# Seven block products in place of eight for the output projection of token tile pairs, in a fused attention and gMLP kernel

## The chip, the cores and the metric

The kernel runs on one core of a Trainium2 chip. Its time is device microseconds of one launch; the median of three runs is compared.

## The reference, cut to what matters

Two blocks follow each other on 2048 tokens of 1024 features. The first is a layer norm, a QKV projection, a sliding attention over eight keys two tokens apart, and an output projection, with a residual. The second is a gated MLP that mixes tokens; the change lies there:

```python
h = x + _A_ref(_layernorm(x), A_wqkv, A_wo)
z = _gelu(einsum('bsd,df->bsf', _layernorm(h), w_in))   # 2 * 1792 features
z1 = z[..., :Fh]
z2 = _layernorm(z[..., Fh:])
g = einsum('ts,bsf->btf', w_sp, z2) + b_sp[None, :, None]
out = h + einsum('bsf,fd->bsd', z1 * g, w_out)          # (2048 x 1792) @ (1792 x 1024)
```

Everything is bf16 at the interface. `w_sp` is 2048 x 2048, `w_out` 1792 x 1024.

## The kernel before

TensorE, ScalarE (ACT), VectorE (DVE) and GpSimd (POOL) run in the order in which the kernel issues their instructions. Up to the last Gelu that order comes from a planner, the class `Order`, which is given operations with estimated costs, dependencies and buffer slots. From there on (line 1087) it is written out by hand, and so is the order of SyncE's (SP) loads.

The planned part makes, among other things, `z1` and the normalised `z2` and stores them in DRAM. `b_z1` (line 851) evicts an accumulator of two PSUM banks through the Gelu on ACT (L867). Three accumulators, tag `acc`, take six of the eight PSUM banks; the attention's pool `ps_att` has the other two. `row_sum` (L899) takes the sums of magnitudes of the rows of `w_sp` on ACT, with an accumulator; `row_scales` (L903 to L908) makes a power of two from each, by which the rows are scaled so that they can be held in fp16, and `rinv`, the factor that undoes it at the end. `load_raw` loads `w_sp` transposed, `scale_raw` (L941) scales it to fp16.

The hand-written part goes over two passes `pr`, each for 1024 output tokens. A pass has a group stage and an output stage.

- Group stage: seven groups `i`, each for two tiles of 128 features. A group makes `g` for them as one 2 x 2 block product with seven instead of eight products. The forms of `w_sp` (sums and differences of blocks) come from `t_forms` (L948 to L954, 4096 elements a partition each), once for each pass; the forms of `z2` from `z_form` (L971, 1024 elements each), four for each group, built on VectorE one group ahead. `times` (L1071) issues eight matmuls of 512 columns; a group has four products into fresh banks `k1`, `k4`, `k3`, `k2`, and three that go on in `k1`, `k4` and `k3`: 56 matmuls. ACT copies the first three out half way (`p1`, `p7`, `p5`); GpSimd adds `p7 + p5` (L1116) and later three more (L1145, L1146, L1150); VectorE makes `u` (L1144) and the rest (L1149 to L1154) and multiplies by `z1`, loaded as `z1c`. The result is `zg`, 14 feature tiles by 1024 tokens, bf16.
- In pass 0 the groups also carry loads: the rows of `w_sp` for pass 1 (`wn`, two buffers), `w_out` in two pieces on GpSimd's queue (`wout_a` in group 4, `wout_b` in group 5), the next z2 (`z2f`), and the transposed `w_sp` of pass 1. In group 5 one transpose on TensorE (L1131) turns the row scales of pass 1.
- Output stage: eight token tiles `il`. Each makes 14 x 2 matmuls of 512 columns of `zg` with `w_out` (`project`, L1169) into two banks; VectorE scales by `rinv`, adds `h` and writes the output tile `hr` (L1172). Pass 0 has `scale_raw`, `t_forms` and `z_form` for pass 1 between the tiles on VectorE. The last tile of pass 1 is cut into 512, 384 and 128 columns.

All banks of this part come from one pool `psq` of eight. TensorE's first matmul in it waits for the last Gelu.

Of the kernel before, what the change touches and what calls it, by code (L numbers as in the profile page):

```python
# [13 lines left out]
I32 = mybir.dt.int32  # L14
# [118 lines left out]
def kernel(  # L133
# [48 lines left out]
    rinv = cpool.tile([P, NT], I32, name="rinv_w")  # L182

# [49 lines left out]
    with tc.manual_schedule(engines={mybir.EngineType.SP}):  # L233
# [10 lines left out]
        dma(csb[:], consts_d.ap()[:, :])  # L244
        load_pair(2)
# [133 lines left out]
    ps_att = att_stack.enter_context(tc.tile_pool(name="ps_att", bufs=1, space=PSUM))  # L379
# [471 lines left out]
    def b_z1(c):  # L851
        for fp in range(NF // 2):
# [12 lines left out]
            def ev(fp=fp):  # L865
                z1s = l1.tile([P, 2, CH], BF16, name="z1s", tag="xn", bufs=4)
                A.activation(z1s[:], G["accy", c, fp][:], ACTF.Gelu_apprx_tanh)  # L867
                last_store[:] = [(A.dma_start if c == NCH - 1 else dma)(z1_d[2 * fp:2 * fp + 2, :, c * CH:(c + 1) * CH].rearrange("f p s -> p f s"), z1s[:])]
# [24 lines left out]
    def load_wn(i, pool, tag, bufs):  # L893
        wn[i] = pool.tile([P, S], BF16, name="wn", tag=tag, bufs=bufs)
        A.dma_start(wn[i][:], B_w_sp[i * P:(i + 1) * P, :])
# [5 lines left out]
    def row_scales(pr):  # L901
        n = slice(pr * TPP, (pr + 1) * TPP)
        V.tensor_tensor(wlim[:, n], wabs[:, n, 0], wabs[:, n, 1], op=ALU.add)  # L903
        V.tensor_scalar(wlim[:, n], wlim[:, n], 2.0 ** -40, 2.0 ** 60, op0=ALU.max, op1=ALU.min)
        V.tensor_scalar(wexp[:, n], wlim[:, n].bitcast(I32), 0x7F800000, None, op0=ALU.bitwise_and)
        V.tensor_scalar(rsc[:, n], wexp[:, n], -1.0, float(266 << 23), op0=ALU.mult, op1=ALU.add)
        V.tensor_scalar(rinv[:, n], wexp[:, n], float(-(12 << 23)), None, op0=ALU.add)
        V.tensor_copy(rsc16[:, n], rsc[:, n].bitcast(FP32))  # L908

# [102 lines left out]
    def close_():  # L1012
        sp_hand.__enter__()
        att_stack.close()
        zpools["z"] = ctx.enter_context(tc.tile_pool(name="zpool", bufs=1, side="right"))

# [5 lines left out]
    rs_ = add("DVE", 1.0, lambda: row_scales(0), [G["avdone", NCH - 1]] + wabs_ops, prio=2.8)  # L1022
# [34 lines left out]
    psq = ctx.enter_context(tc.tile_pool(name="psq", bufs=8, space=PSUM))  # L1057

    for _ in range(7):
        psq.tile([P, CH], FP32, name="bank", tag="bank", bufs=8)  # L1060

    def bank():
        return psq.tile([P, CH], FP32, name="bank", tag="bank", bufs=8)
# [5 lines left out]
    def times(dst, wts, mov, first):  # L1069
        for k in range(HK):  # L1070
            T.matmul(dst[:], wts[:, k, :], mov[:, k, :], start=(first and k == 0), stop=(k == HK - 1), skip_group_check=not first)  # L1071
# [14 lines left out]

    for pr in range(NCH // 2):
# [5 lines left out]
        for i in range(NQ):  # L1093
# [8 lines left out]
            if i == 0:  # L1102
                zg = p2.tile([P, NF, 2 * CH], BF16, name="zg", tag="zg", bufs=1)
            z1c = z1cs[n]
            k1, k4, k3, k2 = bank(), bank(), bank(), bank()
            times(k1, a11, b11, True)
            A.copy(p1[:], k1[:])  # L1107
            times(k4, zs[n, 3], t3, True)
            A.copy(p7[:], k4[:])
            times(k3, zs[n, 1], t1_, True)  # L1110
            A.copy(p5[:], k3[:])
            times(k2, zs[n, 2], t2_, True)
            times(k1, a12, b21, False)
            times(k4, a22, t4_, False)
            times(k3, zs[n, 4], b22, False)
            nc.gpsimd.tensor_tensor(p7[:], p7[:], p5[:], op=ALU.add)  # L1116
            if pr == 0:
# [4 lines left out]
                if i <= 3:  # L1122
                    for t in (TPP + 2 * i, TPP + 2 * i + 1):
                        load_wn(t, p2, "wn", 2)
                if i == 4:
                    dma_w(wout_a[:], wout_view[:, 0:8, :])
                elif i == 5:
                    dma_w(wout_b[:], wout_view[:, 8:NF, :])
                    row_scales(1)
                    rps = psq.tile([P, 2 * CH], BF16, name="rpq", tag="bank", bufs=8)  # L1130
                    T.transpose(rps[0:TPP, 0:P], rsc16[:, TPP:NT], ident[:])  # L1131
                    A.copy(rscT[0:TPP, :], rps[0:TPP, 0:P])
                    A.dma_start(rs_d[TPP:NT, :], rscT[0:TPP, :])
            if i + 1 < NQ:
                for m in (3, 1, 2, 4):
                    z_form(n + 1, m)
            if n + 2 < 2 * NQ:
# [17 lines left out]
            if i == NQ - 2:  # L1155
                for il in range(3):
                    load_hr(2 * pr * TPC + il)
        for il in range(2 * TPC):
            t = 2 * pr * TPC + il
            if pr == 0 and il == 0:  # L1160
                load_raw(3)
                bias_in(1, p2, "z1c", 2)
            if il + 3 < 2 * TPC:
                load_hr(t + 3)
            hr = hrs[t]

            def project(outs, lo, hi, f):
                wt, f0 = (wout_a, f) if f < 8 else (wout_b, f - 8)
                T.matmul(outs, zg[:, f, il * P:(il + 1) * P], wt[:, f0, lo:hi], start=(f == 0), stop=(f == NF - 1))  # L1169

            def finish_(lo, hi, acc):
                V.scalar_tensor_tensor(hr[:, lo:hi], acc[:, 0:hi - lo], rv[:, t:t + 1], hr[:, lo:hi], op0=ALU.mult, op1=ALU.add)  # L1172

            if t < NT - 1:
                acc = [bank(), bank()]
                for f in range(NF):
                    for nh in range(2):
                        project(acc[nh][:], nh * CH, (nh + 1) * CH, f)
                for nh in range(2):
                    finish_(nh * CH, (nh + 1) * CH, acc[nh])  # L1180
                dma(out2d[t * P:(t + 1) * P, :], hr[:])
            else:
                for n, (lo, hi) in enumerate(LAST_COLS):
                    acc = bank()
# [53 lines left out]
```

## Time and profile before

| | us |
|---|---|
| median of 3 runs (lowest, highest) | 701.23 (700.89, 701.79) |
| the profiled execution, its own time | 701.22 |
| its span | 699.4 |
| TensorE matmuls busy | 693.8 |
| VectorE busy | 508.1 |
| ScalarE busy | 276.6 |
| GpSimd busy | 117.6 |

The table's busy times and the span are of one profiled execution; its own time is 1.8 us longer than its span. Where a row is quoted, its first two numbers are start and length in microseconds from the span's start, then come the engine, the line of the kernel, the operation, and what it writes and reads. PE is TensorE, PEld its weight load. In brackets stands how long the engine was idle before it, and what ended that.

### The profile page before, as it was taken

Reading aid. Unit: us, or ns where it says so; the run is one execution under the profiler, and the core shown is the slowest. Engines: PE = TensorE matmul, PEld = TensorE weight load, DVE = VectorE, ACT = ScalarE, POOL = GpSimd, SP = SyncE. Lnnn points to the kernel's source line nnn. Section 1 sums busy time; section 2 is a strip of 40 time slices with the busy share of each in tenths; the row PEclk is TensorE's granted clock in tenths of the full one; section 3 lists DMA queues with packets and bytes.
Section 4 is the critical chain, followed back from the end, with each engine's and each line's share of the span. In section 5 each row is a group of like instructions: output and inputs, shape, how many; then the busy total and the mean of one; then the engine's idle time right before and its main releaser. Section 6 shows DMA issues by size and latency. Waiting matters only on the chain.

```text
span 699.4 us, 8823 instructions
## 1 busy us (share of the span) xinstructions
PE 693.8 (99%) x3427; PEld 359.4 (51%) x3427; DVE 508.1 (73%) x614; ACT 276.6 (40%) x388; POOL 117.6 (17%) x113
## 2 busy tenths in 40 slices
PE   9999999999999999999999999999999999999998
PEld 7766665566645445444444544444444444444444
DVE  6899899999999799997985177556457845564222
ACT  4547652453238876755673642345100012111000
POOL 0100010011110111100301120424420023435000
PEclk9999999999999999999999999999999999999999
DMA  9968597677993679361864996699995125361121
GB/s 326 328 229 239 173 216 254 152 209 234 250 352 146 185 211 256 135 183 38 178 214 123 233 273 191 194 257 249 321 293 157 57 87 153 96 171 65 46 90 46
DMA packets 145193, 133.04 MB, mean 190 GB/s; under 512 B 68672, under 2 KB 117216, under 8 KB 145024
## 3 DMA queue, kind: packets, MB, share of 16 engines
q1 hardware_dynamic: 132688, 88.93, 45.3%
q0 software_dynamic: 7808, 32.97, 16.7%
q10 hardware_dynamic: 4656, 10.59, 4.7%
q8 instruction: 27, 0.44, 0.2%
q14 instruction: 14, 0.11, 0.1%
HBM read 75.24 MB, written 33.10 MB: 155 GB/s over the span
## 4 chain that ended last, share of the span: by engine, by line
PE 99%; ACT 0%; DVE 0%; issue 0%
PE bank L1071 24%; PE acc L461 22%; PE acc L793 14%; PE acc L861 14%; PE bank L1169 14%; PE acc L716 8%; PE acc L303 2%; PE wps L226 1%; PE L L555 0%; PE tpt L299 0%; PE pb L617 0%; ACT z1s L867 0%; ACT xnT L300 0%; DVE hr L1172 0%; PE tpa L299 0%
## 5 line engine op out<-in xcount | busy, mean ns | idle before, releaser
L861 PE MATMUL acc<-hnT,win 128*128 128x512 bf16 x448 | 98.0, 379 | 0.0
L793 PE MATMUL acc<-win,hnT 128*128 128x512 bf16 (+1 forms) x512 | 98.0, 352 | 0.0
L793 PEld LDWEIGHTS <-hnT 128*128 128x128 bf16 x512 | 49.9, 98 | 47.4 <-issue 0.7
L525 DVE TENSOR_TENSOR prod<-qT,kT 128x4096 bf16<-128x4096 bf16 x32 | 72.7, 2283 | 1.4 <-ACT kT L467 1.4
L1169 PEld LDWEIGHTS <-zg 128*128 128x128 bf16 x462 | 44.7, 98 | 52.4
L1071 PEld LDWEIGHTS <-zs 128*128 128x128 f16 x448 | 43.9, 98 | 52.8
L861 PEld LDWEIGHTS <-win 128*128 128x128 bf16 x448 | 43.7, 98 | 52.6 <-issue 0.7
L472 ACT CAST stg<-acc 128x1024 bf16<-128x1024 f32 x36 | 36.4, 1012 | 61.5 <-PE acc L461 52.3
L1107 ACT COPY p<-bank 128x512 f32<-128x512 f32 x14 | 8.2, 586 | 132.0 <-PE bank L1071 129.6
L1172 DVE SCALAR_TENSOR_TENSOR hr<-bank,rinv_w,hr 128x512 bf16<-128x512 f32 (+2 forms) x33 | 22.9, 730 | 51.4 <-PE bank L1169 51.2
L1169 PE MATMUL bank<-wout_a,zg 128*128 128x512 bf16 (+2 forms) x264 | 58.2, 373 | 0.0
L461 PE MATMUL acc<-xnT,wk 128*128 128x512 bf16 x256 | 56.5, 379 | 0.0
L461 PE MATMUL acc<-xnT,wv 128*128 128x512 bf16 x256 | 56.2, 379 | 0.0
L716 PE MATMUL acc<-wo_sb,av_oT 128*128 128x512 bf16 x256 | 56.1, 379 | 0.0
L1071 PE MATMUL bank<-rawa,z2f 128*128 128x512 f16 x224 | 52.9, 379 | 1.1 <-ACT z1s L867 1.1
L1071 PEld LDWEIGHTS <-z2f 128*128 128x128 bf16 x336 | 32.8, 98 | 40.8 <-issue 1.4
L1071 PE MATMUL bank<-rawb,zs 128*128 128x512 f16 x224 | 52.9, 379 | 0.0
L1071 PE MATMUL bank<-form,zs 128*128 128x512 f16 x224 | 50.6, 379 | 0.0
L461 PEld LDWEIGHTS <-wk 128*128 128x128 bf16 x256 | 36.5, 143 | 19.0 <-issue 0.8
L461 PEld LDWEIGHTS <-wv 128*128 128x128 bf16 x256 | 36.5, 144 | 18.7 <-issue 0.5
L1169 PE MATMUL bank<-wout_b,zg 128*128 128x512 bf16 (+2 forms) x198 | 44.4, 373 | 0.0
L867 ACT ACTIVATE z1s<-acc 128x1024 bf16<-128x1024 f32 x28 | 28.6, 1023 | 36.5 <-PE acc L861 32.3
(189 smaller groups left out, 941.6 us busy)
## 6 DMA issues: line engine op xcount, KB each, us to landing
z2f<-z_d SPq DMA_DIRECT2D x28, 512.0 KB, 5.7
qkv_d<-stg SPq DMA_DIRECT2D x36, 256.0 KB, 5.7
wn<-in_B_w_sp_dram ACTq DMA_DIRECT2D x16, 512.0 KB, 4.2
z1c<-z_d SPq DMA_DIRECT2D x14, 512.0 KB, 4.1
z_d<-z1s SPq DMA_DIRECT2D x21, 256.0 KB, 2.3
z_d<-u SPq DMA_DIRECT2D x12, 448.0 KB, 2.5
av_y<-av_z POOLq DMA_DIRECT2D x4, 1024.0 KB, 9.8
av_oT<-av_zz POOLq DMA_DIRECT2D x4, 1024.0 KB, 15.0
```

The lines of the kernel that those rows point to most:

```text
L303: T.matmul(dst.rearrange("p (a b) -> p a b", b=P), wqs[:, kt, dl, :], xnT[0][:, lo:hi, kt, :], start=start, stop=stop)
L461: T.matmul(G[key][:, j, :].rearrange("p (a b) -> p a b", a=TPC), wv[:, kt, dl, :], xnT[c][:, :, kt, :], start=(kt == 0), stop=(kt == KT - 1))
L472: A.copy(stg[:], G[key][:])
L525: V.tensor_tensor(st["prod"][:], qT[:], kT[:, :, o:o + CH], op=ALU.mult)
L716: T.matmul(st["acc", il][:, nh, :], oTs[c][:, dl, il * P:(il + 1) * P], wo_sb[:, dl, nh * CH:(nh + 1) * CH], start=(dl == 0), stop=(dl == ...
L793: T.matmul(accf[:, n0:n1], hnTs[c][:, il, kt, :], wins[hf][:, kt, n0:n1], start=(kt == 0), stop=(kt == KT - 1))
L861: T.matmul(G["accy", c, fp][:, j, :].rearrange("p (a b) -> p a b", a=TPC), wt[:, kt, f0 * P:(f0 + 1) * P], hnTs[c][:, :, kt, :], start=(kt ...
L867: A.activation(z1s[:], G["accy", c, fp][:], ACTF.Gelu_apprx_tanh)
L1071: T.matmul(dst[:], wts[:, k, :], mov[:, k, :], start=(first and k == 0), stop=(k == HK - 1), skip_group_check=not first)
L1107: A.copy(p1[:], k1[:])
L1169: T.matmul(outs, zg[:, f, il * P:(il + 1) * P], wt[:, f0, lo:hi], start=(f == 0), stop=(f == NF - 1))
L1172: V.scalar_tensor_tensor(hr[:, lo:hi], acc[:, 0:hi - lo], rv[:, t:t + 1], hr[:, lo:hi], op0=ALU.mult, op1=ALU.add)
```

## The change

The output product takes the tokens in pairs of tiles and `w_out` in blocks: even and odd feature tiles by two halves of 512 columns. Each pair is then a 2 x 2 block product too, with seven products of seven matmuls (512 columns) instead of eight. Its parts:

- `zg`, `z1c` and `w_out` become fp16. So that they stay in range, each pair of feature tiles gets a power of two: `feature_scales` from sums that the Gelu's accumulator now gives (`zsum`), applied to `z1c` in each group, and undone in `w_out`, which is scaled once (`wout_scaled`: four ACT instructions for `wout_a`, three on VectorE for `wout_b`, 2048 elements each). A level for all of `w_out` is found from sums of magnitudes (`wout_sum`: eight on ACT, six reductions on VectorE, in groups 2 to 4 of pass 0), turned on TensorE in group 5 beside the row scales, and spread by a small matmul between group 5 and group 6.
- `row_scales` also takes the bias into account: `b_sp` is loaded to `rscT` early, turned by one transpose and its magnitude taken on ACT, in the planned part.
- The loads of `w_out` move to groups 0 and 1 of pass 0. The rows `wn` are loaded as pairs into one buffer.
- The forms of `w_out` are made once, in the output stage of pass 0: T1 and T2 on VectorE, T4 on GpSimd, T3 on VectorE in place of a block. The pair before that, pair 0 of pass 0, is still multiplied in full, with 56 matmuls. The forms of `zg`, four for each pair, 896 elements each (`s_form`, tile `sf`), are made on VectorE a pair ahead.
- A pair's products are combined with ACT, GpSimd and VectorE, as in a group.
- The PSUM banks: `k1` of each group and pair comes from a pool of two in the place of the attention's banks (`psA`), the others from a pool of six.

```diff
-                A.activation(z1s[:], G["accy", c, fp][:], ACTF.Gelu_apprx_tanh)
+                A.activation(z1s[:], G["accy", c, fp][:], ACTF.Gelu_apprx_tanh, accum_out=zsum[:, c, fp:fp + 1])
...
+        zpools["ps"] = ctx.enter_context(tc.tile_pool(name="psA", bufs=2, space=PSUM, side="right"))
...
+    psB = ctx.enter_context(tc.tile_pool(name="psB", bufs=6, space=PSUM))
...
+    def wout_scaled(fp):
+        w_ = wout_a[:, 2 * fp:2 * fp + 2, :] if fp < 4 else wout_b[:, 2 * fp - 8:2 * fp - 6, :]
+        if fp < 4:
+            A.activation(w_.bitcast(FP16), w_, ACTF.Copy, scale=kf[:, fp:fp + 1])
+        else:
+            V.tensor_scalar(w_.bitcast(FP16), w_, kf[:, fp:fp + 1], None, op0=ALU.mult)
...
+    def wform(eng, out, x, y, only=(0, 1)):
+        for h in only:
+            eng.tensor_tensor(out[h], x[h], y[h], op=ALU.subtract)
...
+            if pr == 0 and i == 5:
+                row_scales(1)
+                wout_level()
+                turned = bank(BF16)
+                T.transpose(turned[0:TPP, 0:P], rsc16[:, TPP:NT], ident[:])
+                T.transpose(turned[0:1, P:2 * P], kb[:, 0:1], ident[:])
...
-                if i == 4:
+                if i == 0:
                     dma_w(wout_a[:], wout_view[:, 0:8, :])
-                elif i == 5:
+                elif i == 1:
                     dma_w(wout_b[:], wout_view[:, 8:NF, :])
...
+                for f in WSUM.get(i, ()):
+                    wout_sum(f)
+            V.tensor_scalar(z1c, z1cs[n][:], sf[:, i:i + 1], None, op0=ALU.mult)
             if i + 1 < NQ:
                 for m in (3, 1, 2, 4):
                     z_form(n + 1, m)
+            elif pr == 1:
+                for m in (3, 1, 2, 4):
+                    s_form(TPC, m, 0, NQ - 1)
+            else:
+                for fp in range(NQ):
+                    wout_scaled(fp)
+                scale_raw(2, 0)
+                scale_raw(2, HK)
+            if pr == 0 and i == 5:
+                wout_turned(turned[0:1, P:2 * P])
+                wout_spread(bank())
...
+        for q in range(TPC):
...
+            if pr == 0 and q == 0:
...
+                wform(V, T1, B12, B11)
+                wform(V, T2, B22, T1)
+                wform(nc.gpsimd, T4, B21, T2)
+                for m in (3, 1, 2, 4):
+                    s_form(1, m)
+                wform(V, B12, B22, B12)
+                for t, nh, acc in accs:
+                    hr, r_ = (h1, h2)[t], (r1, r2)[t]
+                    V.scalar_tensor_tensor(hr[:, nh * CH:(nh + 1) * CH], acc[:], r_, hr[:, nh * CH:(nh + 1) * CH], op0=ALU.mult, op1=ALU.add)
...
+            prods = ((k1, a11, B11), (k4, S3, T3), (k3, S1, T1), (k2, S2, T2))
...
+            times(k1[:], a12, wslab(B21), False, 0, NQ, NQ)
+            times(k4[:], a22, wslab(T4), False, 0, NQ, NQ)
...
+            nc.gpsimd.tensor_tensor(p7[:], p7[:], p5[:], op=ALU.add)
+            if q + 1 < TPC:
+                for m in (3, 1, 2, 4):
+                    s_form(w + 1, m)
+            elif pr == 0:
+                for m in (3, 1):
+                    z_form(NQ, m)
+                t_forms(1, 1)
+                for m in (2, 4):
+                    z_form(NQ, m)
+            V.tensor_tensor(u[:], k2[:], p1[:], op=ALU.add)
+            A.activation(p1[:], u[:], ACTF.Copy, scale=r1)
+            A.activation(p5[:], u[:], ACTF.Copy, scale=r2)
+            nc.gpsimd.tensor_tensor(p1[:], p1[:], h1[:, CH:D], op=ALU.add)
+            nc.gpsimd.tensor_tensor(p5[:], p5[:], h2[:, 0:CH], op=ALU.add)
+            nc.gpsimd.tensor_tensor(p7[:], p7[:], u[:], op=ALU.add)
+            V.scalar_tensor_tensor(h1[:, 0:CH], k1[:], r1, h1[:, 0:CH], op0=ALU.mult, op1=ALU.add)
+            V.scalar_tensor_tensor(h2[:, 0:CH], k4[:], r2, p5[:], op0=ALU.mult, op1=ALU.add)
+            V.scalar_tensor_tensor(h2[:, CH:D], p7[:], r2, h2[:, CH:D], op0=ALU.mult, op1=ALU.add)
...
+                if q == 1:
                     scale_raw(3, 0)
                     scale_raw(3, HK)
+                elif q == 2:
                     t_forms(1, 0)
                     t_forms(1, 3)
+                else:
                     t_forms(1, 2)
                     bias_rows(1)
```

In the last pair of pass 1 the product into `k3` is cut into 384 and 128 columns.

## The prediction

> **What bounds the kernel now.** The page first: busy times and the shares of the chain that ended last.
>
> ```profile
> PE 693.8 (99%) x3427; PEld 359.4 (51%) x3427; DVE 508.1 (73%) x614; ACT 276.6 (40%) x388; POOL 117.6 (17%) x113
> ...
> PE 99%; ACT 0%; DVE 0%; issue 0%
> ```
>
> TensorE never rests, so every matmul removed pays, if its operands are there in time. Next the chain in order of time (start, length, what), for the part the change touches.
>
> ```profile
> 428.95 1.03 ACT z1s L867
> 429.99 0.04 issue
> 430.03 72.68 PE bank L1071 x336
> 502.71 0.15 PE rpq L1131
> ...
> 515.05 48.35 PE bank L1169 x224
> 563.39 84.61 PE bank L1071 x392
> 648.00 48.40 PE bank L1169 x238
> 696.42 0.35 DVE hr L1172
> ```
>
> One stall, 1.07 us ahead of the first spatial group; then seven groups of 56 matmuls, the first output stage, seven groups, the second output stage. One 512-column matmul costs 48.35/224 = 0.2158 us, a group 12.09 us. Then the windows by stage (PE, PEld, DVE, ACT, POOL busy), for the two output stages:
>
> ```profile
> 515.00:563.30 48.30, 48.30 (x226) 21.88 (x224) 32.40 (x31) 0.00 (x0) 0.00 (x0) 1.00 0.51 137
> 648.00:696.40 48.40, 48.38 (x239) 22.58 (x236) 12.68 (x19) 0.00 (x0) 0.00 (x0) 1.00 0.20 63
> ```
>
> In the first, VectorE already works 32.4 of 48.3 us, since it builds there all that pass 1 needs. The change puts its new work on that engine and on GpSimd. How those two meet is in the timeline:
>
> ```profile
> 345.35 2.29 DVE L641 TENSOR_TENSOR av_p<-vT,AB 128x4096 bf16<-128x4096 bf16 x1
> 345.60 2.92 POOL L685 TENSOR_TENSOR l3rstd<-l3var,nhalf 128x4 f32<-128x4 f32 x1 [1.90 <-DVE l3var L681]
> 347.67 2.29 DVE L649 TENSOR_TENSOR av_b<-av_b,av_p 128x4096 bf16<-128x4096 bf16 x1
> ...
> 460.24 1.30 POOL L1116 TENSOR_TENSOR p<-p,p 128x512 f32<-128x512 f32 x1 [5.86 <-ACT p L1111]
> 460.51 1.57 DVE L971 TENSOR_TENSOR zs<-zs,z2f 128x1024 f16<-128x1024 f16 x1
> ```
>
> The 0.69 us form zs took 1.57: it ended 0.54 after the GpSimd addition, so it began only when that was over. The other way round, L685 (1.02 alone) took 2.92, 1.9 more, which is where the VectorE instruction ended: the waiting engine gets its turn at the other's next instruction boundary.
>
> **Taken away.** 448 output matmuls become 56 + 7 x 49 = 399: 49 x 0.2158 = 10.6 us. The first group's bank: 1.07 us (the next bank is wanted 1.73 later, after the Gelu ended; cover 0.7). Both are on the path. So group 0 starts at 428.95, plus 0.15 for the new bias transpose (as rpq): 429.1. Ahead of that all else is hidden: a read of the accumulator per Gelu (0.19 x 28, ACT 40% busy, two accumulators spare), one 4 KB load. If they were not, they cost 0.19 each.
>
> **Group stage, pass 0.** VectorE gets per group one scaling of z1c (2048 elements; L829's 1792 took 0.745: 0.85) and in groups 2 to 4 two reductions of 1024 (statistics of 512 took 0.64 to 0.69: 1.2 each). Its round is then 2.4 + 0.85 + four forms 2.8 + 6.55 (from u's start, 437.86, to the last product's end, 444.41: the span of GpSimd's three additions) = 12.6 against 12.09: it can't catch up. It starts late: in group 0 the scaling waits for z1c (issued 432.28, 4.1 to landing by the page, then 0.85 and four forms, 2.8), so u moves from 437.86 to 440.0 and the last product to 446.5. In group 1 it waits for z2f, now loaded beside w_out, moved here from groups 4 and 5 (with its two issues on GpSimd's queue, 0.93 and 0.85, which stand between additions that wait for the later u anyway). There the DMA view shows
>
> ```profile
> wout_a<-in_B_w_out_dram POOLq DMA_DIRECT2D x1, 2048.0 KB, 11.2
> ...
> z2f<-z_d SPq DMA_DIRECT2D x2, 512.0 KB, 10.1
> ```
>
> against 5.7 elsewhere. Issued at 439.65, landing 449.75: forms 2.8, then 6.55: 459.1. Groups 2 to 4: +37.8 = 496.9. The row sums of w_sp now share one buffer of two rows: their loads start when the sums of the two before are done, some 10 us into a group, and land 3.8 later, 4 ahead of the next sums. Thirteen small instructions at 0.2 (row scales, level of w_out): 499.5. TensorE wants their transposes 6.9 us into group 5 (429.1 + 60.45 + 6.9 = 496.45): **3.05 us stall**. Without the slower landing VectorE would be there at 497.1, 0.65 late; these are the bounds. Two further transposes beside rpq's and the spread: 0.3. Group 6 starts at 489.55 + 12.09 + 0.45 + 3.05 = 505.1.
>
> **VectorE's queue from there.** It stands at the spread matmul until 505.1, with group 5's evictions behind it. Then, in its order: three small copies 0.6; group 5's evictions 6.55; z1c 0.85, three w_out scalings 2.55, scale_raw 4.48 (L941's two): 520.2; group 6's evictions 6.55: 526.7. TensorE meanwhile has group 6 done at 517.2 and pair 0 (56 matmuls still) at 529.3; its last two features come in time, ACT's four scalings (1.9 each, from 1792 in 1.70) are 0.2 late at most.
>
> Now T1 and T2 (2048 and 1536 elements each, at 1.22 for 2048): 4.3, to 531.0. T4 then takes its turn on GpSimd. Its rate: 512 elements in 1.26 with two 32-bit operands, 1.155 with one of 16 bits, so 1.05 by the same step with two; I take 1.1: 4.4 + 3.3 us. [...] During it VectorE's forms stand still, but for one at the boundary: 4.4 + 0.6 + 3.3 = 539.3; three more forms 1.9: 541.2; T3's first piece 1.22: 542.4, its second 543.3. TensorE has done the one product that needs none of this at 530.8 and waits for T3: **11.6 us stall**.
>
> Behind T3, all before pass 1 can run: four evictions of pair 0 2.8; pair 1: four forms 2.4, its combination 6.3 (u 0.69, ACT 0.59, GpSimd 1.16 + 1.16 + 1.26, two evictions 1.42), scale_raw 4.5; pair 2: 2.4 + 7.3 (the next pair's addition takes GpSimd first), two t_forms 4.6; pair 3: z_forms and t_form 5.0, 7.3, last t_form 2.3. Together 44.9: **588.2**. TensorE, going again from 542.4, has 180 matmuls (38.8) until it wants that last form in group 7 (pass 1's first): idle for 7 more us, in pieces. From there 16 + 336 + 196 = 548 matmuls: 118.3, so its end is 706.5, before 696.4: +10.1. In pass 1 all fits: in its output stage VectorE is busy 12.68 of 48.4 us, and a pair needs 2.4 + 3.5 us of it in 10.6; if a form came late there, it would cost its own 0.6.
>
> **The tail.** The last pair's chain starts with u when 4.5 us of matmuls are left: 0.69 + 0.59 + 1.16 + 1.16 + 1.26 = 4.86, then evictions 0.75, 0.62, 0.35 (L1172): 2.05 after TensorE instead of 0.37: +1.7.
>
> **Sum.** +10.1 + 1.7 = +11.8. It is made against the profiled execution, 701.22 (span 699.4 and 1.8 around it); the median is 701.23. Forecast **713.0**. With the small landing time 710.6, with GpSimd at 1.26 714.1, at 1.05 712.6.
>
> **Rivals.**
> - *Cold restart.* The trace has no long TensorE stall but the start, and there eleven matmuls took
>
> ```profile
> 1.19 4.88 PE L226 MATMUL wps<-warm 128*128 128x512 bf16 x11 [1.19 <-DVE eps_t L229]
> ```
>
> 2.5 us more than eleven at 0.2158, though the windows give PEclk 1.00 there. The stall in pair 1 would hide it, the one in group 7 not: 715.5. [...] Against: group 7's idling is in pieces.
> - *Loads later still.* Before, 431 to 455 moved 4.96 MB; 3.5 MB more makes 354 GB/s, near the 390 to 410 of the best slices. Five us more at z2f go through the full rounds one to one: 718, with a cold restart 720.5.
> - *The engines pass each other*, T4 lying beside VectorE's work. Then 7.7 and some 2 of collisions go: 703.3, and with the small landing time 700.9. The stretched rows speak against it.
> - *Faster: TensorE keeps the pace.* If VectorE has pass 1's last form by 566.6 (429.1, seven groups, 0.45, then 56 + 147 + 40 matmuls: where group 7 wants it), without stalls, only -10.6 - 1.07 + 0.6 + 1.7 is left: 691.8. For it: VectorE idles 15.9 us in that stage now. Against: its queue as summed runs 21.6 us past that point, and without GpSimd's turns still 12.
> - *Not what it says*: none; the order of instructions has 49 fewer full matmuls.
>
> **How the numbers follow.** The queue decides, 0.50 (708 to 715); cold restart 0.18; late loads 0.12; engines pass 0.13 (699 to 704); TensorE keeps the pace 0.07. 702 to 721 leaves out the last case and half of the one before it below, some 0.06 above. A measurement tells about 0.2% (1.4 us) from no change. Faster: 0.07 and a third of "engines pass", 0.11; same 0.04; slower 0.85.
>
> **What would show it.** Right: TensorE idle before the products with T3 by 10 us or so, released by VectorE; form sf on VectorE stretched from 0.6 to about 4; T4 4.4 and 3.3 us; idle time in group 7 before the last form; a late transpose in group 5; no idle time in pass 1; the last eviction 2 us after the last matmul. Wrong: sf at 0.6 beside T4, or T3 done before TensorE's pair 0 ends.

## Result and the profile after

The changed kernel takes **722.6 us** (median of 4 runs, 720.94 to 723.0) against 701.08 us for the kernel before beside it (4 runs); the ratio is 1.030, 95% interval 1.0283 to 1.0318. The forecast was 713.0, range 702 to 721: the direction and the places were right, the size was 9.6 us short, and the time lies 1.6 us above the range. The profiled execution is the shortest of the four: 720.94, a span of 719.2 (before: 699.4).

The page: busy times of the engines, and the shares of the chain that ended last.

```profile
PE 690.4 (96%) x3374; PEld 355.0 (49%) x3374; DVE 568.2 (79%) x706; ACT 316.2 (44%) x472; POOL 164.1 (23%) x143
...
PE 80%; DVE 8%; POOL 4%; issue 4%; DMA 2%; ACT 0%; POOLq 0%; DVEq 0%; SPq 0%
```

TensorE has less to do and is no longer the whole chain. The list of TensorE's waits from 420 us on (what it waited for, total, times, longest) says where it rests:

```profile
PE bank L1091 <- DVE wout_a L1178: 9.6, 1, 9.6
PE bank L1091 <- DVE form L969: 5.2, 1, 5.2
PE bank L1229 <- DVE rsc L918: 4.7, 1, 4.7
PE banka L1091 <- ACT p L1219: 1.3, 1, 1.3
PE bank L1230 <- DVE kb L1145: 0.9, 1, 0.9
```

From above: T3 (pair 1), the last form ahead of group 7's products, and the transposes of group 5: the three places of the forecast. Together with the two small waits 21.7 us; the forecast had 3.05 + 11.6 + 7 = 21.65. The chain in order of time (start, length, what):

```profile
429.18 1.73 PE banka L1091 x8
...
439.97 11.68 DMA z2f<-z_d
...
502.53 3.12 PE banka L1091 x8
505.64 3.45 PE bank L1091 x16
...
530.45 4.09 DVE woutT L1178 x4
534.53 7.82 DVE sf L1194 x2
...
543.58 1.23 DVE wout_a L1178
544.85 6.96 PE bank L1091 x21
...
590.60 2.21 DVE form L969
592.85 5.79 PE bank L1091 x16
```

Eight matmuls take 1.73 us, sixteen 3.45. Behind each of the three waits the same work is slower: eight in 3.12, sixteen in 5.79, and 21 in about 6.8 instead of 4.53. The windows over these stretches (us; busy time of PE, PEld, DVE, ACT, POOL; granted clock; DMA share; GB/s):

```profile
502.46:509.00 6.54, 6.54 (x25) 2.60 (x24) 3.78 (x11) 0.25 (x1) 0.00 (x0) 0.80 0.12 42
544.85:551.65 6.80, 6.80 (x22) 2.54 (x21) 5.14 (x8) 1.17 (x2) 0.65 (x1) 0.66 0.23 82
592.85:598.48 5.63, 5.63 (x17) 2.13 (x18) 5.00 (x8) 0.00 (x0) 0.94 (x1) 0.61 0.36 110
```

The granted clock is 0.80, 0.66 and 0.61 there on average. Taken finer, it is 0.50 from 501.69 to 505.10, from 539.23 to 549.47 and from 590.43 to 597.26 us, and 1.00 between these spells. That is the term which the forecast's likeliest case didn't have. The timeline around T4 (start, length, engine, line, operation):

```profile
533.80 4.64 POOL L1178 TENSOR_TENSOR wT<-wout_a,woutT 128x2048 f16<-128x2048 f16 x1 [5.32 <-DMA brow<-in_B_b_sp_dram]
534.45 7.89 DVE L1194 TENSOR_TENSOR sf<-zg 128x896 f16<-128x896 f16 x2
538.41 3.46 POOL L1178 TENSOR_TENSOR wT<-wout_b,woutT 128x1536 f16<-128x1536 f16 x1
...
545.58 1.40 DVE L1318 SCALAR_TENSOR_TENSOR hr<-bank,rinv_w,hr 128x512 bf16<-128x512 f32 x2
```

Two forms, of a kind that takes 0.62 us each in VectorE's rows at 542.38 and 543.04, take 7.89 beside GpSimd's 4.64 and 3.46: the engines did not pass each other here. The last row is the first eviction of pair 0, which stands behind T3 in VectorE's queue. And the two output stages in the windows, as before:

```profile
521.20:577.20 56.00, 46.30 (x204) 20.30 (x203) 45.43 (x44) 9.31 (x14) 24.78 (x14) 0.91 0.42 118
671.10:713.70 42.60, 42.54 (x204) 19.41 (x201) 24.55 (x37) 12.17 (x20) 18.67 (x16) 1.00 0.21 74
```

The second stage does what the change promises: 42.6 us instead of 48.4, no wait over 0.3 us. The first takes 56.0 for 203 full matmuls (43.8 us of work): VectorE, with 45.4 us of instructions and its waits for GpSimd, sets its length.

### The profile page after: what moved, and what is told of

It reads as the page before. It is cut to its first block, busy times and chain, and to the rows that moved or that the text cites. A ratio compares the mean times of both kernels' runs of the same rounds, so it can differ in the third digit from the quotient of the medians.

```text
span 719.2 us, 8962 instructions
## 1 busy us (share of the span) xinstructions
PE 690.4 (96%) x3374; PEld 355.0 (49%) x3374; DVE 568.2 (79%) x706; ACT 316.2 (44%) x472; POOL 164.1 (23%) x143
## 3 DMA queue, kind: packets, MB, share of 16 engines
q1 hardware_dynamic: 132720, 88.93, 43.8%
## 4 chain that ended last, share of the span: by engine, by line
PE 80%; DVE 8%; POOL 4%; issue 4%; DMA 2%; ACT 0%; POOLq 0%; DVEq 0%; SPq 0%
PE acc L464 21%; PE bank L1091 16%; PE acc L796 13%; PE acc L864 13%; PE acc L719 8%; PE banka L1091 6%; PE acc L306 2%; DMA z2f<-z_d 2%; DVE sf L1194 1%; DVE zs L988 1%; POOL zg L1278 1%; POOL u L1274 1%; POOL p L1273 1%; DVE small L1136 1%; DVE zg L1280 1%
## 5 line engine op out<-in xcount | busy, mean ns | idle before, releaser
L475 ACT CAST stg<-acc 128x1024 bf16<-128x1024 f32 x36 | 36.4, 1012 | 61.6 <-PE acc L464 48.4
L1091 PE MATMUL banka<-rawa,z2f 128*128 128x512 f16 x224 | 54.2, 386 | 1.3 <-ACT p L1219 1.3
L803 ACT ACTIVATE u<-acc 128x1024 bf16<-128x1024 f32 (+1 forms) x32 | 29.3, 915 | 30.7 <-PE acc L796 30.7
L1219 ACT COPY p<-banka 128x512 f32<-128x512 f32 x14 | 8.1, 581 | 78.0 <-PE banka L1091 75.7
L464 PE MATMUL acc<-xnT,wq 128*128 128x512 bf16 x192 | 41.9, 379 | 0.0
L719 PEld LDWEIGHTS <-av_oT 128*128 128x128 bf16 x256 | 24.9, 98 | 30.0
L532 DVE TENSOR_TENSOR prod<-prod 128x2048 bf16<-128x2048 bf16 x32 | 38.7, 1215 | 0.0
```

Of the source, the lines that this page charges most:

```text
L464: T.matmul(G[key][:, j, :].rearrange("p (a b) -> p a b", a=TPC), wv[:, kt, dl, :], xnT[c][:, :, kt, :], start=(kt == 0), stop=(kt == KT - 1))
L475: A.copy(stg[:], G[key][:])
L532: V.tensor_tensor(dst, p_[:, 0:4, :], p_[:, 4:8, :], op=ALU.add)
L719: T.matmul(st["acc", il][:, nh, :], oTs[c][:, dl, il * P:(il + 1) * P], wo_sb[:, dl, nh * CH:(nh + 1) * CH], start=(dl == 0), stop=(dl == ...
L803: A.activation(st["u", il][:, hf * 1024:hf * 1024 + wd], G["accz", c, il, hf][:].rearrange("p a b -> p (a b)")[:, 0:wd], ACTF.Gelu_apprx_t ...
L1091: T.matmul(dst, wts(k), mov(k), start=(first and k == 0), stop=(k == last - 1), skip_group_check=not first)
```

## Experiments

Times are medians; the kernel before lay between 701.08 and 701.31 beside them. "Profiled" compares the spans of profiled executions, with 719.2 for the changed kernel.

**1. T4 on VectorE.**

```diff
-                wform(nc.gpsimd, T4, B21, T2)
...
                 wform(V, B12, B22, B12)
+                wform(V, T4, B21, T2)
```

> The changed kernel with one edit: the form T4 of w_out is computed on VectorE right behind T3 instead of on GpSimd ahead of the four forms sf. Theory (the two engines shut each other out): T2 still ends near 534.5, the four sf take 0.62 each, T3's first piece ends near 538.3 and TensorE waits some 3 us for it instead of 9.65; T4 adds 2.2 us to VectorE, which then has everything behind it 4.2 us sooner; so the last form ahead of group 7 moves from 592.8 to about 588.5 and the time from 722.6 to about 718.4. Rival A (the sf waited for something else, their operands or their buffers): they still take 8 us and T4's 2.2 us on VectorE come on top, 724.8. Rival B (TensorE's wait for T3 is itself the price, VectorE's queue is not): the whole 6.5 us come back, 716.

Measured: 715.05 us (714.97 to 715.55), profiled 713.2. In the timeline of this run the two forms that took 7.89 take 1.15, and TensorE's wait for T3 falls to 2.91:

```profile
534.51 1.15 DVE L1194 TENSOR_TENSOR sf<-zg 128x896 f16<-128x896 f16 x2
...
538.16 1.02 PE L1091 MATMUL bank<-wout_a,sf 128*128 128x512 f16 x4 [2.91 <-DVE wout_a L1178]
...
540.90 1.40 DVE L1318 SCALAR_TENSOR_TENSOR hr<-bank,rinv_w,hr 128x512 bf16<-128x512 f32 x2
...
587.70 3.30 PE L1091 MATMUL bank<-form,z2f 128*128 128x512 f16 x8 [5.23 <-DVE form L969]
```

So the theory holds for the mechanism: VectorE stands at pair 0's evictions at 540.90 instead of 545.58, 4.7 sooner (forecast 4.2), and the last form is done 5.2 sooner. TensorE's own 6.7 us at T3 do not come back: it waits the same 5.23 us for the last form. Profiled it is -6.0: 5.2 from the last form, and the sixteen matmuls behind that wait lose 1.4 here instead of 2.2. By its median alone the run lies nearer to rival B (716) than to the theory (718.4); what speaks against the rival is that the wait for the last form is unchanged and comes 5.2 sooner, as VectorE's queue does.

**2. The bank part alone**, on the kernel before:

```diff
-    psq = ctx.enter_context(tc.tile_pool(name="psq", bufs=8, space=PSUM))
+    psq = ctx.enter_context(tc.tile_pool(name="psq", bufs=6, space=PSUM))
...
+        zpools["ps"] = ctx.enter_context(tc.tile_pool(name="psA", bufs=2, space=PSUM, side="right"))
...
-            k1, k4, k3, k2 = bank(), bank(), bank(), bank()
+            k1, k4, k3, k2 = bank_a(), bank(), bank(), bank()
```

> The kernel before with the bank part of the change alone: a pool of two banks in the place that attention gave up, the first product of each group (and one of the two accumulators of each output tile) in it, six banks for the rest. Theory: the 1.07 us stall ahead of the first group goes and nothing takes its place, since the next bank is wanted 1.73 us later, when the last Gelu has been over for 0.7 us: about 700.1. Rival (the next bank or six banks in the output stage bring a wait of their own): 701.1 or above.

Measured: 700.0 us against 701.26, ratio 0.9981 (0.9973 to 0.9990). Nothing waits in its place: the list of TensorE's waits from 420 us on is empty. This part is worth 1.26 us in the medians, where 1.07 was forecast.

**3. TensorE kept busy in group 7.**

```diff
+            if pr == 1 and i == 0:
+                for r in range(3):
+                    times(k4[:], slab(a11), slab(b11), True)
             times(k4[:], slab(zs[n, 3]), slab(t3), True)
```

> The changed kernel with 24 extra matmuls in group 7 (the first group of pass 1), which repeat the group's first product into the bank of the second one, whose own first matmul overwrites them; their operands are there, so they run in the stretch in which TensorE waited 5.23 us for the last form. They take 5.18 us. Theory (the sixteen matmuls behind that wait took 5.79 us instead of 3.45 because TensorE had rested): with TensorE kept busy they take 3.45, the rest of the kernel moves up by 2.3, time 720.3. Rival (they are slow for another reason: operands just written, VectorE and GpSimd reading beside them): they still take 5.8, time 722.6, or 1 to 2 us more where the extra matmuls start late.

Measured: 718.76 us (718.63 to 718.80), profiled 717.0. In its timeline:

```profile
592.87 1.90 PE L1091 MATMUL bank<-form,z2f 128*128 128x512 f16 x8 [0.98 <-DVE form L969]
...
594.60 1.89 PE L1091 MATMUL bank<-rawb,zs 128*128 128x512 f16 x8
```

The last form comes at the same moment as in the changed kernel (592.87 against 592.85), and 24 useless matmuls more make the kernel faster: the sixteen behind the wait take 3.46 us instead of 5.79. The profiled executions differ by 2.2, as expected; the medians by 3.8. The other three runs of the changed kernel, 1.4 to 2.1 above its profiled one, have no trace; their mean granted clock is on record, 0.982 against 0.984.

**4. w_out's loads back in groups 4 and 5**, the sums of magnitudes taken over other data of the same size.

```diff
+        src = raw[0][:, 2 * (f % 8):2 * (f % 8) + 2, :].bitcast(FP16).rearrange("p a b -> p (a b)")
...
-                if i == 0:
+                if i == 4:
                     dma_w(wout_a[:], wout_view[:, 0:8, :])
-                elif i == 1:
+                elif i == 5:
                     dma_w(wout_b[:], wout_view[:, 8:NF, :])
```

> The changed kernel with the two loads of w_out moved back to groups 4 and 5, where the kernel before has them; the fourteen absolute sums stay on their engines and in their groups, but are taken over parts of the first spatial operand of the same size, since w_out is not there yet (so the level of w_out is another power of two). Theory (the stall of group 5 comes from z2f of group 2's operands landing 11.7 us after their issue, beside w_out): they land some 5 us sooner, VectorE's round stays at 12.6, its transposes come near 497, the stall of group 5 shrinks from 5.5 to about 0.7 and no cold restart follows; group 6 starts near 502.7 instead of 509.1 and all behind it moves with VectorE's queue: about 716.3. Rival A (the longer round with the sums makes the stall): transposes still after 500, 721 or more. Rival B (VectorE's queue behind group 6 does not hang on group 5): stall gone, time within 2 us of 722.6.

Measured: 714.87 us (713.59 to 715.46), profiled 713.5. Waits of TensorE:

```profile
PE bank L1091 <- DVE wout_a L1179: 9.7, 1, 9.7
...
PE bank L1230 <- DVE rsc L918: 0.3, 1, 0.3
```

z2f of group 2 is there at 446.6 instead of 451.75, the transposes come at 496.5 instead of 501.2, and the wait of group 5 is 0.3 instead of 4.7. Group 6 starts at 503.1, 6.0 sooner, and the profiled time falls by 5.7 while the later waits stay as they were: VectorE's queue carries every microsecond of group 5 to the end. The theory holds (716.3 was expected), and both rivals fall.

**5. The sums on ScalarE, the loads left early.**

```diff
-        if f < 8:
+        if True:
             A.activation(zg[:, NF - 1, :], wout_tile(f), ACTF.Abs, accum_out=l1n[:, f:f + 1])
```

> The changed kernel with the six absolute sums of w_out that VectorE takes in groups 2 to 4 given to ScalarE as well; w_out is loaded in groups 0 and 1 as in the changed kernel. Theory (VectorE starts late into group 1 for the landing of z2f and can't catch up only because its round is as long as TensorE's): the round falls by 2.1 us in each of the three groups, VectorE is back in time for the transposes of group 5, the stall of 4.7 us there shrinks below 1, no cold restart, and the time comes out as with the loads moved back, 714.5 to 716. Rival (the round has other waits, on GpSimd and on the loads of groups 2 to 4, so that the time saved is lost again): stall of 2 us or more, 718 to 722.

Measured: 712.99 us (712.31 to 715.75), profiled 711.2; the median is 1.5 below the expected range. The starts of u in groups 1 to 4:

```profile
453.52 0.68 DVE L1272 TENSOR_TENSOR u<-bank,p 128x512 f32<-128x512 f32 x1
...
465.11 0.68 DVE L1272 TENSOR_TENSOR u<-bank,p 128x512 f32<-128x512 f32 x1
...
476.05 0.68 DVE L1272 TENSOR_TENSOR u<-bank,p 128x512 f32<-128x512 f32 x1
...
487.13 0.68 DVE L1272 TENSOR_TENSOR u<-bank,p 128x512 f32<-128x512 f32 x1
```

z2f of group 2 lands as late as in the changed kernel (VectorE takes its second half at 451.32), and yet no wait is left in group 5: VectorE has made up for it in the next three rounds, u following u in 11.6, 10.9 and 11.1 us instead of 12.7, 12.5 and 13.2 in the changed kernel (from 453.95 to 492.45). So the stall of group 5 needed two things together, the late landing and a round without slack to recover from it; taking either away is enough.

**6. Seven products in pass 1 alone.** Pass 0 and its output stage are those of the kernel before (with the bank of experiment 2); the forms of w_out are made during pass 1, whose groups leave VectorE some 4.7 of 12.1 us.

```diff
+                for f in range(*((0, 7), (7, NF))[i]) if i < 2 else ():
+                    wout_sum(f)
...
+                if i == 3:
+                    wout_spread(spread)
+                if i in (3, 4):
+                    for fp in ((0, 1, 4, 5) if i == 3 else (2, 3, 6)):
+                        wout_scaled(fp)
+                if i == 5:
+                    wform(V, T1, B12, B11)
+                    wform(V, T2, B22, T1)
+                if i == NQ - 1:
+                    wform(V, B12, B22, B12)
```

> A new version: pass 0 and its output stage as in the kernel before (56 matmuls per pair, bf16, w_out loaded in groups 4 and 5), seven products in pass 1 alone; w_out's sums on ScalarE in groups 0 and 1 of pass 1, its scalings in groups 3 and 4, T1 and T2 on VectorE in group 5, T3 in group 6, T4 behind it; the bank of the first group as in the changed kernel; in the last pair one of the three GpSimd additions goes to VectorE. Theory (a matmul left out pays where VectorE has time for the forms: 7.4 of 12.1 us busy in a group of pass 1, 11.7 with T1 and T2): 28 matmuls less are 6.04 us, the bank 1.07, against 0.4 for transposes and the spread and about 1 for the tail: 695.4. Rival A (VectorE comes late in group 5 or 6 of pass 1, whose rounds then hold 11.5 to 12 us): up to 3 us of stall and a cold restart, 698 to 701. Rival B (fewer matmuls save nothing, something else sets the end): 700 or more.

Measured: 703.3 us (701.85 to 703.67, nine runs), ratio 1.0027 (1.0017 to 1.0037): 0.3% slower than the kernel before, and above the 698 to 701 of rival A too, whose mechanism the trace shows: new waits,

```profile
PE bank L1218 <- DVE kb L1151: 2.9, 1, 2.9
PE banka L1091 <- DVE zg L1291: 1.3, 1, 1.3
```

the first because the spread matmul stands at the head of a group and VectorE has the group before's evictions ahead of what it needs, the second because T3 was put ahead of group 6's evictions. TensorE still ends at 694.3, 2.1 sooner than in the kernel before, but the last store ends 5.8 us after it instead of 3.0. The last pair's loads of hr also came late (GpSimd waited 2.1 us for them). The trace is of one of the two shortest runs. These two, at a mean granted clock of 1.000 and 0.999, took 701.9 us; the other seven, at 0.995 to 0.997, took 703.0 to 703.7. So the wait of 2.9 us, after which the trace shows full clock (1.00 from 601.71 to 608.70), may have had a price in the others; they have no trace.

**7. The same with these waits taken out** (comments for the reader).

```diff
+                if 1 <= il <= 4:                      # output stage of pass 0
+                    for f in range(4 * il - 4, min(4 * il, NF)):
+                        wout_sum(f)
...
+                if i in (0, 1):                       # groups of pass 1
+                    for fp in ((0, 1, 4, 5) if i == 0 else (2, 3, 6)):
+                        wout_scaled(fp)
+                if 2 <= i <= 5:
+                    wform(V, *((T1, B12, B11), (T2, B22, T1), (B12, B22, B12), (T4, B21, T2))[i - 2])
...
+            if end:                                   # last pair
+                V.scalar_tensor_tensor(h2[:, CH:D], p7[:], r2, h2[:, CH:D], op0=ALU.mult, op1=ALU.add)
+                V.tensor_tensor(p5[:], p5[:], h2[:, 0:CH], op=ALU.add)
```

> The version with seven products in pass 1 alone, its new waits taken out: the sums of w_out on ScalarE and its level in the output stage of pass 0, the spread matmul in the middle of group 0 of pass 1, scalings in groups 0 and 1, one form T each in groups 2 to 5 on VectorE, the next pair's hr loaded at the head of a pair, and in the last pair two of GpSimd's three additions on VectorE with the stores in the order in which they are ready. Theory: the version before it lost 2.9 us at the spread and 1.3 at the last features of group 6, and its last store ended 5.8 us after TensorE instead of 3.0; without them the 28 matmuls (6.04) and the bank (1.07) are left against 0.5 for transposes and 0.5 at the end: 695.1. Rival (each wait taken out is replaced by the next on VectorE's queue, whose groups of pass 1 hold 9.6 to 11.9 of 12.1 us): 698 or more.

Measured: **696.18 us** (695.91 to 696.79), ratio 0.9924 (0.9913 to 0.9936): faster than both kernels. Windows of pass 0's output stage, pass 1's groups and pass 1's output stage:

```profile
513.98:562.50 48.52, 48.52 (x226) 21.91 (x225) 34.08 (x43) 9.02 (x18) 0.00 (x0) 1.00 0.52 139
562.58:647.30 84.72, 84.72 (x394) 38.36 (x393) 63.16 (x89) 20.00 (x25) 31.80 (x26) 1.00 0.41 115
647.39:690.00 42.61, 42.61 (x204) 19.43 (x201) 27.85 (x41) 12.18 (x20) 20.06 (x17) 1.00 0.19 62
```

TensorE is busy throughout and ends at 690.0, 6.4 before the kernel before: the 28 matmuls left out and the bank, less some small ones. Its end is still 4.5 us ahead of the last store's, 1.5 more than before, where 0.5 was expected; that is nearly all of the 1.1 us by which the expectation was missed.

**8. Experiments 1 and 4 together.**

> The changed kernel with both edits that were run one at a time: the form T4 on VectorE behind T3, and the loads of w_out back in groups 4 and 5 with the sums taken over other data. Theory (both move the same queue, VectorE's, and add): 722.6 - 7.5 - 7.7 = 707.4, and at least 705, since VectorE's work of the first output stage and the longer end remain. Rival (each took away a part of the same waiting): 712 or more.

Measured: 709.66 us (709.0 to 710.51), ratio 1.0117. The medians don't add up, but the profiled executions do: 719.2 less 6.0 and 5.7 is 707.5, and 707.5 was measured. The expectation took the gains from medians, and with them twice the 1.7 us by which the changed kernel's median lies above its profiled run.

**9. TensorE kept busy in all three stalls**: to experiment 3 come (comments for the reader)

```diff
+                for r in range(2):                                    # group 5, ahead of the transposes
+                    times(turned[:].bitcast(FP32), slab(a11), slab(b11), True)
...
+                for r in range(6 if w == 1 and k_ is k4 else 0):      # pair 1, ahead of the products with T3
+                    times(k4[:], a11, wslab(B11), True, 0, NQ, NQ)
```

> The changed kernel with extra matmuls in all three stretches in which TensorE waits: 16 ahead of the transposes of group 5 (into their bank, which they overwrite), 42 ahead of the products with T3 in pair 1 and 24 in group 7 (as in the run with group 7 alone), all repeats of a product whose operands are there, into banks that the next matmul begins anew. Theory (the matmuls behind each stall are slow because TensorE had rested, some 6 us in all three places: 1.4 in group 5, 2.3 in pair 1, 2.3 in group 7): all three runs of matmuls take 0.216 us each; group 5's 1.4 us move VectorE's queue at the spread matmul, pair 1's are partly hidden behind VectorE; the time falls below the 718.8 of the run with group 7 alone by 1.4 to 2.5: 716.3 to 717.4. Rival (only the stall of group 7 has such a price): 718.8; the matmuls behind the other two stalls stay slow.

Measured: 719.16 us (716.97 to 719.90), no better than experiment 3, as the rival had it, but not for its reason. Behind the first two stalls the matmuls now run at full pace and the last form is done at 591.04, 1.8 sooner; but TensorE came to group 7 earlier, used up the 24 extra matmuls and rested again, 3.36 us, and the sixteen behind it took 6.38 us at a granted clock of 0.53:

```profile
591.09:597.47 6.38, 6.38 (x16) 2.24 (x17) 5.50 (x9) 0.00 (x0) 1.61 (x2) 0.53 0.47 138
```

**10. The repairs together** (experiments 5, 1 and 3, and two of the last pair's additions on VectorE), seven products still in both passes.

> The changed kernel, seven products in both passes, with the repairs together: all sums of w_out on ScalarE, T4 on VectorE behind T3, the 24 extra matmuls in group 7, and in the last pair two of GpSimd's three additions on VectorE. Theory (what is left of the change's price is VectorE's queue between group 5 and the last form ahead of group 7, which TensorE waits for): 713.0 - 5.2 for T4 - 2.3 to 3.8 for group 7 - 1 at the end = 703.0 to 704.5, so still slower than the kernel before, and the seven products of pass 0 cost some 7 us against the version with pass 1 alone. Rival (the repairs overlap, as two of them did in part): 706 or more. Rival (without stalls the 49 matmuls come through): below 700.

Measured: 707.5 us (706.63 to 710.15), ratio 1.0096. Waits of TensorE:

```profile
PE bank L1091 <- DVE form L969: 4.8, 1, 4.8
PE bank L1091 <- DVE wout_a L1178: 2.9, 1, 2.9
PE bank L1233 <- POOL p L1239: 1.0, 1, 1.0
```

The first rival: the 24 extra matmuls were used up before the last form here too, 4.8 us of rest were left, and the sixteen took 5.1 us (1.7 to be had). Without that loss the kernel would still be 9.6 us behind experiment 7. Of this, 8.7 us are the three waits above: VectorE's queue is still late at T3 and at the last form, and group 5's second transpose waits 1.0 (VectorE's `kb` ended just before it, at 497.26).

**11. As experiment 9, with 40 extra matmuls in group 7.**

> The run with extra matmuls in all three stalls, with 40 instead of 24 of them in group 7, since TensorE came there sooner and still rested 3.4 us after them, and the sixteen matmuls behind that took 6.4 us. Theory (a rest of a few us anywhere ahead of a matmul makes the next ones slow, and what remained above 717 was this): the last form ends at 591.0 as in that run, TensorE waits under 1 us for it, the sixteen take 3.45 us, profiled time 716.9, the runs closer together than 1 us (they lay between 717.0 and 719.9). Rival (the extra matmuls themselves hold up VectorE or ScalarE, or the slow matmuls have another cause): 719 or more, or the sixteen matmuls still slow.

Measured: 716.97 us (716.89 to 717.02), profiled 715.2. The profiled run's own time is 717.01, where 716.9 was expected. The three stretches of the first section, in this run:

```profile
502.52:507.80 5.28, 5.28 (x25) 2.27 (x24) 3.83 (x11) 0.26 (x1) 0.00 (x0) 1.00 0.18 62
543.65:548.19 4.54, 4.54 (x22) 2.05 (x22) 4.52 (x7) 1.17 (x2) 0.65 (x1) 1.00 0.18 64
591.14:594.59 3.45, 3.45 (x17) 1.57 (x16) 3.25 (x5) 0.00 (x0) 0.14 (x1) 1.00 0.36 118
```

6.54 became 5.28, 6.80 became 4.54, 5.63 became 3.45, at a clock of 1.00 in all three, with the same operands and the same work of VectorE beside them. So it is the rest that makes them slow, and the slowed clock costs the changed kernel 722.6 - 717.0 = **5.6 us** of its 21.5 in the medians. Between the profiled executions it is 4.0 (719.2 less 715.2), since the changed kernel's other runs are longer than its profiled one.

These figures are near, not exact. In this run the last form was done at 590.16 already, 0.8 sooner than expected: one of VectorE's evictions, which took 1.73 us beside a GpSimd addition in the changed kernel (588.20), took 0.75. TensorE came to the form only at 591.14, when its extra matmuls ran out. The two nearly cancel, so that the hit at 716.9 is in part luck.

## Why the prediction was right or wrong

Step by step, in us of the span:

| step | forecast | measured |
|---|---|---|
| group 0 starts | 429.1 | 429.18 |
| u of group 0 | 440.0 | 440.46 |
| z2f of group 2 there | 449.75 | 449.96 and 451.75 (halves) |
| first transpose of group 5 | 499.5 | 501.19 |
| group 6 starts | 505.1 | 509.13 |
| T2 done | 531.0 | 534.54 |
| T4's two pieces | 4.4, 3.3 | 4.64, 3.46 (each with a wait in it) |
| T3's first piece done | 542.4 | 544.80 |
| last form done | 588.2 | 592.80 |
| TensorE ends | 706.5 | 713.67 |
| last eviction after that | 2.05 | 2.1 |
| span | 711.2 | 719.2 |

**Right:** the bank (experiment 2 alone), VectorE's queue as what decides, the three stalls with their releasers, VectorE standing still beside GpSimd's T4 (7.89 us for two forms, 1.15 in experiment 1), pass 1 without stalls behind its first group, the last eviction 2 us behind TensorE. That the stalls' lengths add up to what was forecast (21.7 against 21.65) is luck: one by one they are 5.5 for 3.05 (group 5), 9.65 for 11.6 (T3) and 6.5 for 7 (group 7).

**The step that failed is the price of a stall.** The forecast counted each as idle time and nothing more. The runs showed 1.3 to 2.3 us of slow matmuls behind each in the changed kernel, and 5.6 us of its median in all: without them the time, 717.0, is inside the range. A restart at a lower clock was there as a rival with 2.5 us, for group 7 alone, at a chance of 0.18, and was turned down with "group 7's idling is in pieces". It was in one piece of 5.23 and one of 1.28. The other argument, that the stall in pair 1 would hide a restart, failed for group 5: VectorE itself stood at the spread matmul, behind 24 matmuls of which the first eight were slow, so that 1.3 us went into its queue. Over the sixteen matmuls behind rests of 3.4 to 5.2 us the clock was 0.53 to 0.70, and they took 1.4 to 2.9 us more than at full clock. In the changed kernel's trace the clock falls from 1.00 to 0.50 each time, but at no fixed delay: 5.2 us after TensorE's rest began in group 5 (496.52 to 501.69, with one transpose between), 4.0 at T3 (535.20 to 539.23) and 2.8 in group 7 (587.62 to 590.43). It stayed at 0.50 for 2.6, 4.6 and 4.4 us of the work behind.

**Terms that were mis-sized**, about 4.0 us together (the span without slowed matmuls is experiment 11's 715.2, against 711.2):
- z2f's second half landed 1.9 us later than forecast (1.8 after the first), and two small chains ended late in group 5: the first transpose 1.7 later than summed, and the second waited 0.86 for the level of w_out. The forecast had one stall there, for both transposes.
- Between T3 and the last form 48.0 us went by where 45.8 were summed. Pair 1's forms for pair 2 took 4.5 instead of 2.4, since VectorE waited 1.9 for buffers that TensorE's late products held (in experiment 11, with these products at full pace, it didn't wait and they took 3.5, so that part of this is the slow clock again); pair 2's took 3.7, since GpSimd's addition (L1342, 3.07 instead of 1.26) and the forms met again.
- From T2 to T3's first piece it took 10.3 us where 11.4 were summed, since T4 itself is some 0.85 shorter than forecast (by the estimate in the last section), and 0.5 less from group 6's start to T2; these go the other way.
- The end: 5.5 us from TensorE's end to the span's, before 3.0; the forecast had 1.7 more instead of 2.5. The evictions were right; from the last of them to the end it is 3.4 us instead of 2.6. Four stores are issued there within a microsecond (715.05 to 715.91), which may be why; no run tells.

The median lies 1.7 us above the profiled execution, where the forecast had 0.0. Its runs spread by 2.1 us. Those of experiments 4, 5, 8, 9 and 10, which rest ahead of group 7 too, spread by 1.9, 3.4, 1.5, 2.9 and 3.5; where that rest is filled (3 and 11) the spread is 0.17 and 0.13. Experiment 1 rests there and spreads by 0.58 only. The mean granted clock, on record for every run, is lower in the longer runs of the changed kernel and of experiments 6, 9 and 10, but doesn't go with the time in 1 and 5. So it is likely from these numbers, but not shown, that the spread comes from how long the lower clock lasts.

**The other rivals.** "Engines pass each other" fell with the row of 7.89. "TensorE keeps the pace" is not the changed kernel's case, but it is experiment 7's: where VectorE has the forms in time, the matmuls left out pay in full. "Loads later still" had the price right (a late landing goes through the rounds) at 1.9 us instead of 5. One row was read loosely: the 1.02 us of L685 alone is the row of the same operation at L427, while L685's own shortest rows are 1.38; the argument doesn't hang on it.

## What to carry to other kernels

Here matmuls left out paid only in the stage where the engine that has to prepare for them had time to spare: the same seven products cost 21.5 us when both passes had them, and gained 5.1 us with the bank when the forms were built during pass 1's groups. Behind TensorE's waits of 3.4 to 9.65 us the matmuls lost 1.3 to 2.9 us more in the changed kernel and in experiments 1, 9 and 10, so count such a wait at its own length plus that, and ask for each piece whether it is contiguous; a stall in an engine that others wait for passes that on (group 5's 1.3 us went into VectorE's queue). A load that is moved earlier has to be charged to what then lands beside it (z2f's second half was there at 451.75 beside w_out, at 446.6 in experiment 4), and a loop whose helper engine has a round as long as the loop's did not recover here from one late start (12.5 to 13.2 us a round beside groups of 12.1).

## What the runs showed of the hardware

- The length of rest that lowers the clock: no drop after 0.98 and 1.30 us (experiment 3, sixteen matmuls in 3.46; experiment 11, clock 1.00), nor after 2.94 us in experiment 6's profiled run (1.00) and the 2.9 us ahead of T3 in experiments 8 (T1's and T2's matmuls at a mean of 379 ns, as a full one has in the kernel before) and 10 (1.00 from 500 to 580.89), but there was one around the 2.91 us ahead of T3 in experiment 1, where seven matmuls ran at 0.83 and the next fourteen took 4.58 us instead of 3.02 (0.68). So a rest of 2.9 us can go either way, and the drop may come after the work has begun again: by the two means, 0.83 from 538.16 to 539.97 and 0.68 from there to 544.39, the clock fell there at about 539.4, 1.2 us after TensorE had started (an estimate, with spells at 0.50 as in the changed kernel's trace).
- In the changed kernel's trace the granted clock is 1.00 or 0.50 from the first group on, and up to the end of TensorE's work its three spells at 0.50 last 3.41, 10.24 and 6.83 us: one, three and two times 3.41. The stretches at 1.00 between them, 34.1 and 41.0 us, are ten and twelve times as long. So the changes in this trace lie on a raster of 3.41 us. That the price of a rest depends on where it falls on it would fit, but no run shows it alone: the same 5.23 us ahead of group 7 cost 2.2 us in the changed kernel (sixteen matmuls in 5.63 instead of 3.45) and 1.4 in experiment 1 (in 4.86).
- GpSimd's subtractions with two 16-bit operands have rows of 4.64 us for 2048 elements and 3.46 for 1536, but each row holds a wait for VectorE, whose instruction ahead of it ended at 534.54 and at 538.92. From there to the ends of the rows (538.44 and 541.87) are 3.90 and 2.95 us, 1.9 ns an element: an estimate from these rows, if GpSimd's work began only there; no run has T4 on GpSimd with VectorE at rest. The 32-bit additions of 512 take 1.26, 2.46 ns each, so by that estimate narrow operands help there somewhat more than the forecast's 1.1 us per 512; VectorE does the same 2048 in 1.22.
